# An identity tile built on VectorE, and weight sums taken from tiles that are still on the chip

## Chip, cores and metric

The kernel runs on one core of a Trainium2 chip. The metric is the device time of one execution in microseconds (us), as the median of several runs. The engines are TensorE (PE; its weight loads are listed as PEld), VectorE (DVE), ScalarE (ACT), GpSimd (POOL) and SyncE (SP), which here only issues DMAs. Every engine works through its instructions in order.

## What is computed

An attention with a feature map, and behind it two feed-forward networks. Cut to what matters:

```python
def _attn_ref(q, k, v, w_phi):          # q, k, v: (4, 8, 576, 64), w_phi: (64, 128)
    def phi(x):
        proj = np.einsum('bhsd,df->bhsf', x, w_phi)
        proj = proj - np.max(np.abs(proj), axis=-1, keepdims=True)
        return np.concatenate([np.exp(proj), np.exp(-proj)], axis=-1)
    q_p, k_p = phi(q), phi(k)
    kv = np.einsum('bhsf,bhsd->bhfd', k_p, v)
    z = np.sum(k_p, axis=2)
    num = np.einsum('bhsf,bhfd->bhsd', q_p, kv)
    den = np.einsum('bhsf,bhf->bhs', q_p, z)[..., None] + 1e-06
    return num / den
# x = attention output as (2304, 512)
r = np.maximum(x @ w_in, 0.0)                      # first network, w_in (512, 2048)
x = (r * r) @ w_out                                # w_out (2048, 512)
gate = 1.0 / (1.0 + np.exp(-(x @ w_gate)))         # second network, w_gate, w_val (512, 1536)
out = gate * (x @ w_val) @ w_out2
```

The inputs `moe_w_in`, `moe_w_out` and so on arrive as 64-bit floats; the kernel makes 32-bit ones of them on the chip ("conversion").

## The kernel before

*Attention* (`actx`, lines 213 to 484). Sixteen iterations `n`, each for a batch and a pair of heads. Tiles of q, k and v are loaded on SP's queue two to three iterations ahead (`load`, L261 to L269, and for the last 64 rows of k and v `load_rem`, L251, L255), transposed on PE with the tile `ident` as the moving operand (`trans_q` L292, `trans_k` L285, `trans_rem` L300), projected (`proj_q` L313, `proj_k` L334), and multiplied. The maximum over the features of q is taken by POOL's `partition_all_reduce` (L318), and used on DVE by `q_exp` (L324).

Before the first iteration (lines 223 to 245) `make_identity` makes `ident` on POOL, with a fill (masks.py:197) and a select (masks.py:199). `w_phi` is loaded on ACT's queue, split into `wq` and spread into `wk` on DVE (L96, L97, L231 to L241). Then PE runs eight matmuls of `ident` by itself (L245), whose result nobody reads, and the transposes of the first iteration follow.

*First network.* 2304 tokens are three blocks of 768. The first block is computed straight (lines 787 to 806, steps `s` = 0 to 17): `h0_step(s)` makes hidden chunk `s` (L517; ACT L520 to L522, DVE L523: a high and a low half, `ghi` and `glo`), and `o1_step(0, s-2)` adds chunk `s-2` into the output (L538). Every fp32 product is made of three passes over high and low halves. A chunk's weights come from DRAM into a `wf` tile (`fetch`, L197; six buffers, fetched two steps ahead) and are split on ACT (L138) and DVE (L139) into `hl`.

The other blocks use a Strassen-Winograd scheme (`chain`, L590): it needs, beside the weights, four sums of each pair of weight pieces (`s1` to `s4`), which lie in DRAM in `wsm` (`ismd`), one tile for two pairs.

*Conversion* (`weight`, lines 105 to 118; `convert1`, 144 to 150). A piece is loaded as 64-bit data on SP (L108, 512 KB), made into a 32-bit tile `a` on DVE (L112, L113, L114, L117) and ACT (L116), in one of four buffers `wpa`, and stored to DRAM on SP: a piece of `w_in` into `half` (L147, `wid`), a piece of `w_out` into `parked` (L133, `wd`). The order is in, in, out, out for each pair. Ten pieces are converted during the attention (`CONVERTING`): the input pieces 0 to 5 and the output pieces 0 to 3. The rest follow in steps 0 to 12 of the first block (`converts1`), at 7 pieces for 4 steps.

*Sums* (`sums`, lines 159 to 167; `in_sums`, 169 to 178). For each of eight pairs of input pieces, in steps 3, 5, ..., 17, `in_sums` fetches both pieces back from DRAM into two `wf` tiles (L176), makes the four sums on DVE (L163 to L166) in the one buffer `s`, and stores them on SP (L167). For the second network `convert2` already makes its sums from the converted tiles, kept in `kept` until the pair is there.

*What sets the order.* The code is written in program order; a scheduler then puts each engine's instructions in order by a timeline simulation of its own. `tc.issue_after(last_g[0].ins)` places what is traced inside it behind the latest `glo` (or similar) on that instruction's engine.

Of the kernel before, what the change touches and what calls it, by code (L numbers as in the profile page):

```python
# [9 lines left out]

F32 = mybir.dt.float32
# [3 lines left out]
ALU = mybir.AluOpType  # L15
# [5 lines left out]
def attention_moe_moe2(ctx, tc, q, k, v, w_phi, w_in, w_out, w_gate, w_val, w_out2, out):  # L21
    nc = tc.nc
# [3 lines left out]
    P = 128  # L26
# [11 lines left out]
    C1 = w_in.shape[1] // P  # L38
# [5 lines left out]
    CONVERTING = (1, 2, 3, 4, 5, 6, 7, 8, 10, 12)  # L44
# [8 lines left out]
    wpa = ctx.enter_context(tc.tile_pool(name="wpa", bufs=NWA))  # L53
# [30 lines left out]
    def col_src(w, c):  # L84
        return w[:, c * P:(c + 1) * P].rearrange("(j p) f -> p j f", p=P)

    def row_src(w, c):
        return w[c * P:(c + 1) * P, :].rearrange("p (j f) -> p j f", j=NJ)
# [16 lines left out]
    def weight(pool, src):  # L105
        a = pool.tile([P, NJ * P], F32, tag="w", name="w")
        st = raw.tile([P, NJ, P], src.dtype, tag="st", name="st")
        nc.sync.dma_start(out=st, in_=src)  # L108
        u = st.rearrange("p j f -> p (j f)").bitcast(U32).rearrange("p (n t) -> p n t", t=2)
        lo, hi = u[:, :, 0], u[:, :, 1]  # L110
        b = a.bitcast(U32)
        nc.vector.tensor_scalar(b, hi, 3, 0x3FFFFFF8, ALU.logical_shift_left, ALU.bitwise_and)  # L112
        nc.vector.scalar_tensor_tensor(b, hi, 0xC0000000, b, ALU.bitwise_and, ALU.bitwise_or)  # L113
        nc.vector.scalar_tensor_tensor(b, lo, 29, b, ALU.logical_shift_right, ALU.bitwise_or)  # L114
        h = hi.bitcast(F32)
        nc.scalar.activation(h, h, AF.Square)  # L116
        nc.vector.scalar_tensor_tensor(a, h, TINY, a, ALU.is_ge, ALU.mult)  # L117
        return a
# [4 lines left out]
    wsm = [dr.tile([P, 4, 2, HF], F32, tag=f"is{q}", name="ismd") for q in range(C1 // 4)]  # L123
    parked = {}

    def in_piece(c):
        q, r = divmod(c, 4)
        return half[2 * q + r % 2][:, r // 2]

    def park(key, a):  # L130
        if key not in parked:
            parked[key] = dr.tile([P, NJ * P], F32, tag=f"d{len(parked)}", name="wd")
        nc.sync.dma_start(out=parked[key], in_=a)  # L133
# [10 lines left out]
    def convert1(k):  # L144
        o, c = order1[k]
        if o == "in":
            nc.sync.dma_start(out=in_piece(c), in_=weight(wpa, col_src(w_in, c)))  # L147
        else:
            park(("o1", c), weight(wpa, row_src(w_out, c)))
        done.add((o, c))  # L150

    done = set()
    gvd = [dr.tile([P, 2, NJ * P], F32, tag=f"gv{c}", name="gvd") for c in range(C2)]
    smd = [dr.tile([P, 4, 2, HF], F32, tag=f"sm{p}", name="smd") for p in range(C2 // 2)]
    order2 = [(c, o) for p in range(C2 // 2) for o in range(2) for c in (2 * p, 2 * p + 1)]
    order2 += [(c, 2) for c in range(C2)]
    kept = {}

    def sums(a, b, dst):
        a11, a12, a21, a22 = a[:, :HF], a[:, HF:], b[:, :HF], b[:, HF:]  # L160
        t = sp.tile([P, 4, HF], F32, tag="s", name="s")
        eng = nc.vector.tensor_tensor
        eng(t[:, 0], a21, a22, ALU.add)  # L163
        eng(t[:, 1], t[:, 0], a11, ALU.subtract)
        eng(t[:, 2], a11, a21, ALU.subtract)
        eng(t[:, 3], a12, t[:, 1], ALU.subtract)  # L166
        nc.sync.dma_start(out=dst, in_=t)  # L167

    def in_sums(i):
        q, m = divmod(i, 2)  # L170
        ab = []
        for k in range(2):
            c = 4 * q + 2 * m + k
            assert ("in", c) in done
            t = wf.tile([P, NJ * P], F32, tag="wf", name="wf")
            nc.sync.dma_start(out=t, in_=in_piece(c))  # L176
            ab.append(t)
        sums(*ab, wsm[q][:, :, m])
# [21 lines left out]
    def fetch_for(s):  # L200
        if s < C1:
            assert {("in", s), ("out", s)} <= done
            fetch(("in", s), in_piece(s))
            fetch(("out", s), parked["o1", s])

    def split_in(s):
        if s < C1 and ("in", s) not in ws:
            wsplit(("in", s), fetched.pop(("in", s)))

    def split_out(s):  # L210
        wsplit(("out", s), fetched.pop(("out", s)))

    with ExitStack() as actx:
        cst = actx.enter_context(tc.tile_pool(name="cst", bufs=1))
# [6 lines left out]
        sm = actx.enter_context(tc.tile_pool(name="sm", bufs=2))  # L221

        ident = cst.tile([P, P], F32, name="ident")
        make_identity(nc, ident)
        wst = cst.tile([P, F], F32, name="wst")
        for e in range(2):
            nc.scalar.dma_start(out=wst[e * D:(e + 1) * D, :], in_=w_phi)
# [10 lines left out]
        for x in range(2):  # L238
            for e in range(2):
                sl = slice(e * D, (e + 1) * D)  # L240
# [268 lines left out]
    def h0_step(c):  # L509
        w = ws.pop(("in", c))  # L510
        gs[c] = pair()
        pp = dbl()
        for i, (o, n) in enumerate(HALVES):
            k = 0
            for j in range(NJ):
                for x, y in passes:
                    nc.tensor.matmul(pp[:, i, :n], lhsT=w[:, x, j, :], rhs=xs[j][:, y, o:o + n], start=k == 0, stop=k == 3 * NJ - 1)  # L517
                    k += 1
        r, sq = scr(), scr()
        nc.scalar.activation(r, pp[:, :, :NH], AF.Relu)  # L520
        nc.scalar.activation(gs[c][0], flat(r), AF.Square)
        nc.scalar.activation(sq, r, AF.Square)  # L522
        last_g[0] = nc.vector.tensor_tensor(gs[c][1], flat(sq), f(gs[c][0]), ALU.subtract)  # L523
# [31 lines left out]
    def xop(t, k):  # L555
        def h(d, j):
            return xy[t, d][:, :, j * NH:(j + 1) * NH]

        def minus(x, y):
            d = scr()  # L560
            nc.vector.tensor_tensor(d, x, y, ALU.subtract)
            return d

        with tc.issue_after(last_g[0].ins):
            if k == "T2":
                diff["T1"] = minus(h(0, 1), h(0, 0))
                src = diff["T2"] = minus(h(1, 1), diff["T1"])
            elif k == "T3":
                src = minus(h(1, 1), h(0, 1))
            elif k == "T4":  # L570
                src = minus(h(1, 0), diff.pop("T2"))
            elif k == "T1":
                src = diff.pop("T1")
            else:
                src = h(*{"B11": (0, 0), "B21": (1, 0), "B22": (1, 1)}[k])
            i = HOME.index(k)
            a = (xp if i < 4 else xb).tile([P, 2, 2, NH], F32R, tag=f"xo{i}", name="xs")
            split(a[:, 0], a[:, 1], src, nc.scalar)
        xs[k] = a
# [174 lines left out]
    def run_ahead(k, nf, nsp):  # L754
        nonlocal done_f, done_s
        while done_f < min(len(seq), k + nf):
            fetch(seq[done_f][0], seq[done_f][1]())
            done_f += 1
        while done_s < min(len(seq), k + nsp, done_f):
            key = seq[done_s][0]  # L760
            wsplit(key, fetched.pop(key))
            done_s += 1
# [6 lines left out]
    def converts1(s):  # L769
        nonlocal nc1  # L770
        with tc.issue_after(last_g[0].ins):
            while nc1 < min(NW1, nw + (7 * (s + 1) + 3) // 4):
                convert1(nc1)
                nc1 += 1
# [3 lines left out]
    def converts2(at):  # L778
        nonlocal nc2
        upto = int(NW2 * (at + 6) / (moe2 + 36))  # L780
        with tc.issue_after(last_g[0].ins):
            while nc2 < min(upto, NW2):
                convert2(nc2)
                nc2 += 1

    fetch_for(1)
    for s in range(C1 + 2):
        if s < C1:
            fetch_for(s + ahead)
            h0_step(s)  # L790
            split_in(s + 1)
        if 1 <= s <= C1:
            split_out(s - 1)
        for i, k in ((C1 - 5, "B11"), (C1 - 4, "B21"), (C1 - 3, "T2"), (C1 - 1, "T3"), (C1 - 1, "T1"), (C1, "B22"), (C1, "T4")):
            if s == i:
                xop(1, k)
        if s >= C1 - 1:
            run_ahead(0, 5, 0 if s < C1 else 3)
        if s >= 2:
            o1_step(0, s - 2, ws.pop(("out", s - 2)))  # L800
        if s < C1:
            converts1(s)
        if s >= 3 and s % 2 and s <= C1 + 1:
            for i in range(C1 // 2):
                if i == (s - 3) // 2:
                    in_sums(i)

    for k, (at, fn, *args) in enumerate(acts):
        run_ahead(first[k], 11, 6)
        fn(*args)  # L810
        converts2(at)
# [30 lines left out]
```

## Time and profile before

| | |
|---|---|
| median of three runs | 1026.83 us (1023.62 to 1028.88) |
| the profiled execution | 1027.08 us, span 1025.3 us |
| PE busy | 992.4 us, 97% of the span |
| PEld, DVE, ACT, POOL busy | 85%, 73%, 59%, 11% |
| HBM read, written | 127.99 MB, 33.03 MB |
| chain of work that ended last | PE 85%, DVE 6%, DMA 4%, ACT 2%, issue 2% |

The span runs from the first to the last instruction; all times below are counted from its start. A busy share is a share of the span. In the timeline a row gives start, duration, engine, line, operation, tiles and shapes, and in brackets how long the engine had stood before it and what ended that. Waits are put down to the release that came last. "<-issue" is time in which the engine waited for nothing that the profile shows.

### The profile page before, as it was taken

To read this page: it belongs to the slowest core of one execution; us is meant where nothing else is said; L and a number is where in the kernel's file an instruction comes from. 1 tells how busy PE (TensorE), PEld (TensorE's weight loads), DVE (VectorE), ACT (ScalarE), POOL (GpSimd) and SP (SyncE) were. 2 spreads that over 40 slices of the span, in tenths; PEclk is the share of its full clock that TensorE was granted. 3 is DMA by queue.
4 is the path that set the end of the run, shared out by engine and by line. 5 is a ranking of instruction groups with operands and counts; after the bars stand their busy time and mean duration, and the time that the engine had idled before them with its cause. 6 is when DMAs were issued, how large, how long until landed. Compare 5 with 4: busy or idle time off the path is not lost.

```text
span 1025.3 us, 17544 instructions
## 1 busy us (share of the span) xinstructions
PE 992.4 (97%) x6488; PEld 870.3 (85%) x6488; DVE 746.6 (73%) x1283; ACT 601.0 (59%) x1081; POOL 109.4 (11%) x198
## 2 busy tenths in 40 slices
PE   5999999999999899999999999999999999999996
PEld 5666666599999799889998899998899988899985
DVE  4799999869875797887968869866566656566542
ACT  4988888546545487545875457654465544455431
POOL 3555665400000000000000000000000000000000
PEclk9999999999999899999999999999999999999999
DMA  8345421339876478457584565642354422544302
GB/s 225 103 142 153 144 92 46 124 119 352 286 270 211 160 246 267 154 167 243 187 282 160 175 187 175 198 139 73 89 158 133 125 93 62 154 133 124 103 13 61
DMA packets 117846, 162.18 MB, mean 158 GB/s; under 512 B 12928, under 2 KB 75008, under 8 KB 117760
## 3 DMA queue, kind: packets, MB, share of 16 engines
q1 hardware_dynamic: 117120, 160.20, 49.8%
q8 instruction: 51, 0.84, 0.3%
q10 hardware_dynamic: 640, 0.85, 0.2%
q14 instruction: 35, 0.29, 0.1%
HBM read 127.99 MB, written 33.03 MB: 157 GB/s over the span
## 4 chain that ended last, share of the span: by engine, by line
PE 85%; DVE 6%; DMA 4%; ACT 2%; issue 2%; POOL 0%; ACTq 0%; SPq 0%; POOLq 0%; DVEq 0%
PE d L590 37%; PE d L538 17%; PE d L694 15%; PE d L517 4%; PE a L360 3%; DMA wf<-wid 2%; PE a L397 2%; PE a L334 2%; PE a L367 1%; PE a L390 1%; PE a L313 1%; DMA st<-in_moe_w_in_dram 1%; PE a L292 1%; DVE km L339 1%; PE a L377 1%
## 5 line engine op out<-in xcount | busy, mean ns | idle before, releaser
L590 PE MATMUL d<-xs,hl 128*128 128x384 f32 x2184 | 385.5, 337 | 3.6 <-ACT c L596 3.6
L590 PEld LDWEIGHTS d<-xs,hl 128*128 128x128 f32 x2184 | 379.5, 188 | 6.7 <-ACT c L596 4.9
L139 DVE TENSOR_TENSOR hl<-wf,hl 128x512 fp32r<-128x512 f32 x282 | 192.5, 688 | 76.4 <-ACT hl L138 75.3
L138 ACT ACTIVATE hl<-wf 128x512 fp32r<-128x512 f32 x282 | 174.9, 625 | 94.4 <-PE d L590 47.5
L538 PE MATMUL d<-ghi,hl 128*128 128x256 f32 (+1 forms) x768 | 191.9, 340 | 0.0
L538 PEld LDWEIGHTS d<-ghi,hl 128*128 128x128 f32 x768 | 133.0, 190 | 16.4
L538 PE MATMUL d<-glo,hl 128*128 128x512 f32 (+1 forms) x384 | 130.0, 342 | 5.1 <-DVE glo L523 5.1
L694 PE MATMUL d<-hl,ghi 128*128 128x512 f32 x432 | 126.7, 395 | 0.0
L94 ACT ACTIVATE ghi<-G 128x768 fp32r<-128x768 f32 x48 | 40.7, 847 | 99.3 <-PE d L694 56.0
L694 PEld LDWEIGHTS d<-hl,ghi 128*128 128x128 f32 x432 | 80.9, 188 | 18.2
L97 DVE TENSOR_TENSOR glo<-G,ghi 128x768 fp32r<-128x768 f32 x48 | 46.0, 958 | 57.3 <-ACT ghi L94 56.9
L596 ACT ACTIVATE c<-d 128x768 f32<-128x768 f32 x78 | 61.3, 809 | 44.7 <-PE d L590 44.5
L318 POOL PARTITION_ALL_REDUCE m<-qe x64 | 82.5, 1359 | 28.5 <-ACT qe L316 26.8
L538 PEld LDWEIGHTS d<-glo,hl 128*128 128x128 f32 x384 | 73.1, 190 | 14.1 <-DVE glo L523 5.4
L619 DVE TENSOR_TENSOR c<-c,d 128x768 f32<-128x768 f32 x54 | 51.2, 953 | 41.1 <-ACT c L596 26.8
L694 PE MATMUL d<-hl,glo 128*128 128x512 f32 x216 | 76.3, 395 | 0.0
L517 PE MATMUL d<-xs,hl 128*128 128x384 f32 x384 | 69.2, 337 | 2.1 <-DVE u L417 1.7
L517 PEld LDWEIGHTS d<-xs,hl 128*128 128x128 f32 x384 | 66.6, 188 | 3.8 <-DVE u L417 2.2
L116 ACT ACTIVATE st<-st 128x512 f32<-128x512 f32 x68 | 45.7, 680 | 37.0 <-DVE w L113 34.2
L694 PEld LDWEIGHTS d<-hl,glo 128*128 128x128 f32 x216 | 40.6, 188 | 9.8
L113 DVE SCALAR_TENSOR_TENSOR w<-st,w 128x512 uint32<-128x512 uint32 x68 | 48.0, 718 | 0.3
L117 DVE SCALAR_TENSOR_TENSOR w<-st,w 128x512 f32<-128x512 f32 x68 | 46.3, 687 | 1.4 <-ACT st L116 0.5
(105 smaller groups left out, 1128.3 us busy)
## 6 DMA issues: line engine op xcount, KB each, us to landing
wf<-wd SPq DMA_DIRECT2D x84, 256.0 KB, 3.0
wf<-smd SPq DMA_DIRECT2D x72, 256.0 KB, 3.0
st<-in_moe_w_out_dram SPq DMA_DIRECT2D x28, 512.0 KB, 5.0
wf<-wid SPq DMA_DIRECT2D x56, 256.0 KB, 4.6
wf<-gvd SPq DMA_DIRECT2D x54, 256.0 KB, 3.1
st<-in_moe_w_in_dram SPq DMA_DIRECT2D x16, 512.0 KB, 5.1
wf<-ismd SPq DMA_DIRECT2D x32, 256.0 KB, 3.5
wd<-w SPq DMA_DIRECT2D x28, 256.0 KB, 3.3
```

The costliest lines, as they stand in the source:

```text
L97: last_g[0] = nc.vector.tensor_tensor(lo, src, f(hi), ALU.subtract)
L113: nc.vector.scalar_tensor_tensor(b, hi, 0xC0000000, b, ALU.bitwise_and, ALU.bitwise_or)
L117: nc.vector.scalar_tensor_tensor(a, h, TINY, a, ALU.is_ge, ALU.mult)
L138: nc.scalar.activation(d[:, 0], a, AF.Copy)
L139: nc.vector.tensor_tensor(d[:, 1], a, f(d[:, 0]), ALU.subtract)
L318: nc.gpsimd.partition_all_reduce(m, a[:, 1, :], channels=P, reduce_op=bass_isa.ReduceOp.absmax)
L517: nc.tensor.matmul(pp[:, i, :n], lhsT=w[:, x, j, :], rhs=xs[j][:, y, o:o + n], start=k == 0, stop=k == 3 * NJ - 1)
L538: nc.tensor.matmul(acc[j][i], lhsT=w[:, x, j, :], rhs=a[y][:, o:o + n], start=c == 0 and k == 0 and (i == 0 or j % 2 == 0), stop=c == C1 - ...
L590: nc.tensor.matmul(acc[k, q][:, m], lhsT=w[:, i, 2 * m + kt, :], rhs=v[:, j, kt, :], start=start and n == 0, stop=n == 5, skip_group_check ...
L596: nc.scalar.activation(side[name, q], acc["X", q], AF.Copy)
L619: nc.vector.tensor_tensor(a, a, acc[k, q], ALU.add)
L694: nc.tensor.matmul(acc[u], lhsT=g[x][:, u * P:(u + 1) * P], rhs=w[:, y].rearrange("p j f -> p (j f)"), start=c == 0 and n == 0, stop=c == ...
```

## The change

Two things are changed. `ident` is no longer made on POOL. On DVE it is filled with zeros; a ramp 0 to 31 is made along the free dimension by five additions, each doubling what is there; `transpose` turns it within blocks of 32x32, so that each row holds its own number; a comparison of the two gives an identity of 32x32 in each group of 32 partitions; and four copies put these on the diagonal of `ident`.

And in the first network, when the second piece of a pair of input pieces is converted inside `converts1` (from the eleventh conversion on), `sums` is called at once with the two converted tiles, and the pair is marked as done. Only pairs that are not done are still made by `in_sums`, now in steps 2, 4, 6 and 8.

```diff
-from concourse.masks import make_identity
@@ convert1
         if o == "in":
-            nc.sync.dma_start(out=in_piece(c), in_=weight(wpa, col_src(w_in, c)))
+            a = weight(wpa, col_src(w_in, c))
+            nc.sync.dma_start(out=in_piece(c), in_=a)
+            kept[c] = a
+            if k >= len(CONVERTING) and c % 2:
+                sums(kept[c - 1], a, wsm[c // 4][:, :, c % 4 // 2])
+                done.add(("sum", c // 2))
         else:
             park(("o1", c), weight(wpa, row_src(w_out, c)))
         done.add((o, c))
@@
         ident = cst.tile([P, P], F32, name="ident")
-        make_identity(nc, ident)
+        ramp = cst.tile([P, 3, 32], F32, name="ramp")
+        nc.vector.memset(ident, 0.0)
+        nc.vector.memset(ramp[:, 0, 0:1], 0.0)
+        for n in (1, 2, 4, 8, 16):
+            nc.vector.tensor_scalar(ramp[:, 0, n:2 * n], ramp[:, 0, :n], float(n), None, ALU.add)
+        nc.vector.transpose(ramp[:, 1], ramp[:, 0])
+        nc.vector.tensor_tensor(ramp[:, 2], ramp[:, 0], ramp[:, 1], ALU.is_equal)
+        for i in range(4):
+            sl = slice(32 * i, 32 * i + 32)
+            nc.vector.tensor_copy(ident[sl, sl], ramp[sl, 2])
@@ the loop over the steps s
-        if s >= 3 and s % 2 and s <= C1 + 1:
-            for i in range(C1 // 2):
-                if i == (s - 3) // 2:
-                    in_sums(i)
-
+        if s in (2, 4, 6, 8) and ("sum", s // 2 - 1) not in done:
+            in_sums(s // 2 - 1)
+
+    kept.clear()
```

## Rows read from the trace of the kernel before

**Rows 1.** Stages: length, busy us of PE, PEld, DVE, ACT, POOL; clock, DMA, GB/s.

```profile
100.00:203.90 103.90, 101.07 (x1158) 63.76 (x1156) 92.76 (x208) 80.54 (x196) 58.99 (x115) 1.00 0.33 104
203.90:278.00 74.10, 73.74 (x422) 69.68 (x423) 59.49 (x106) 39.58 (x59) 0.00 (x0) 1.00 0.73 252
278.00:338.00 60.00, 59.64 (x339) 54.81 (x337) 38.09 (x65) 30.54 (x45) 0.00 (x0) 1.00 0.72 231
...
341.00:348.00 7.00, 4.90 (x16) 4.22 (x17) 6.69 (x10) 3.09 (x4) 0.00 (x0) 0.51 0.80 260
```

**Rows 2.** PE's waits after 200 us: us in total, times, longest.

```profile
PE d L590 <- ACT c L596: 3.6, 4, 0.9
```

**Rows 3.** Timeline of the start.

```profile
0.80 0.09 DVE L231 MEMSET ones<- 128x32 f32 x1 [0.80 <-PEq L826]
0.86 0.17 DVE L233 MEMSET zr<- 128x128 f32 x1
...
2.16 0.75 SPq L251 DMA_DIRECT2D kr<-in_k_dram  x1
...
4.92 0.45 SPq L264 DMA_DIRECT2D k<-in_k_dram  x1
...
9.43 0.28 POOL masks.py:199 TENSOR_SCALAR_AFFINE_SELECT ident<-ident 128x128 f32<-128x128 f32 x1 [8.51 <-issue]
...
9.76 3.74 PE L245 MATMUL a<-ident 128*128 128x128 f32 x16 [9.76 <-POOL ident masks.py:199]
...
13.34 0.66 PE L292 MATMUL a<-ident,q 96*128 96x96 f32 x6
...
13.84 0.60 PE L285 MATMUL a<-ident,k 128*128 128x128 f32 x4
...
16.00 4.95 POOL L318 PARTITION_ALL_REDUCE m<-qe  x4 [6.29 <-ACT qe L316]
...
17.83 0.66 PE L292 MATMUL a<-ident,q 96*128 96x96 f32 x6
...
19.26 0.45 DVE L324 TENSOR_TENSOR qe<-qe,m 128x288 f32<-128x288 f32 x1
```

**Rows 4.** Timeline at the end of the first network's first block.

```profile
332.53 0.83 ACT L521 ACTIVATE ghi<-c 128x768 fp32r<-128x768 f32 x1
...
333.83 0.43 DVE L163 TENSOR_TENSOR s<-wf 128x256 f32<-128x256 f32 x1 [4.00 <-DMA wf<-wid]
...
339.54 0.42 DVE L163 TENSOR_TENSOR s<-wf 128x256 f32<-128x256 f32 x1 [4.16 <-DMA ismd<-s]
...
342.10 0.95 DVE L523 TENSOR_TENSOR glo<-c,ghi 128x768 fp32r<-128x768 f32 x1
...
343.10 0.80 PE L538 MATMUL d<-glo,hl 128*128 128x512 f32 x1 [5.07 <-DVE glo L523]
```

**Rows 5.** Chain that ended last: start, us, what; two stretches of 21 matmuls.

```profile
343.10 6.02 PE d L538 x21
...
470.06 3.65 PE d L538 x21
```

**Rows 6.** DVE groups by shape: busy us, mean ns, idle before.

```profile
L401 DVE STREAM_TRANSPOSE den<-a 128x288 f32<-128x288 f32 x16 | 7.6, 475 | 1.2 <-PE a L390 1.1
L403 DVE TENSOR_SCALAR rd<-den 128x9 f32<-128x9 f32 x16 | 2.6, 165 | 0.1
```

**Rows 7.** DMA issues from 2.1 to 5.35 us: count, KB, median us to landing.

```profile
k<-in_k_dram SPq DMA_DIRECT2D x1, 256.0 KB, 4.7
kr<-in_k_dram SPq DMA_DIRECT2D x1, 128.0 KB, 5.0
```

**Rows 8.** Timeline: the splits for one step, and PE's use of them.

```profile
245.47 1.29 DVE L139 TENSOR_TENSOR hl<-wf,hl 128x512 fp32r<-128x512 f32 x2
...
247.53 4.33 PE L517 MATMUL d<-xs,hl 128*128 128x384 f32 x24
```

**Rows 9.** DMA issues from 204 to 345 us, the stores of the sums.

```profile
ismd<-s SPq DMA_DIRECT2D x8, 512.0 KB, 4.6
```

More of the change, by code (lines that the diff above doesn't have):

```diff
@@ L152, in attention_moe_moe2 @@
     done = set()
+    kept = {}
     gvd = [dr.tile([P, 2, NJ * P], F32, tag=f"gv{c}", name="gvd") for c in range(C2)]
@@ L156, in attention_moe_moe2 @@
     order2 += [(c, 2) for c in range(C2)]
-    kept = {}
     def sums(a, b, dst):
```

## The prediction

> **What bounds the kernel now.** I read the stages first: busy time of each engine in stretches of the span. In each of them TensorE (PE) is close to full: 101.07 of 103.9 us late in the attention, 73.74 of 74.1 in the first network up to 278 us, 59.64 of 60 up to 338 [rows 1]. So nothing is gained by making VectorE (DVE) or the queues cheaper as such; a gain must come from a place where PE stands still. The second view is therefore the list of PE's waits. After 200 us it holds one large entry, at 343 us; the next is four waits at L590 with 3.6 us in sum, which the change does not touch [rows 2]. Before 200 us the large one is the very start, where PE waits 9.76 us for the identity tile. I then read the timeline around both.
>
> *The start.* POOL fills the tile at once, but its select (the second half of the identity) starts only at 9.43 us, after 8.5 us in which POOL waits for nothing that the profile shows; PE's warm-up matmuls (L245) start at 9.76 and take 3.74 us, and the first transposes follow at 13.34 without a gap [rows 3]. The 16 warm-up passes take 234 ns apiece, four transposes of the same shape just behind them 150 ns [rows 3]: they are the price of raising the clock, and come wherever PE starts.
>
> *The end of the first network's first block.* PE stops at 338.03 and takes up L538 at 343.10, after 5.07 us, for the low half of the last hidden chunk (`glo`, L523). Its input was ready on ScalarE (ACT) by 333.36 (332.53 plus 0.83), but on DVE's in-order queue two weight-sum groups (L163) stand ahead of it, one held 4.00 us by its reloaded tile, the next 4.16 us by the landing of the previous sums, which still occupy the single `s` buffer [rows 4]. During the stop the granted clock falls: it is 0.51 over 341 to 348 us, so mostly the lower of the two levels, 1.2 GHz [rows 1]. The 21 matmuls after the stop take 6.02 us, 21 like them elsewhere 3.65 [rows 5].
>
> **Part 1, the identity on DVE.** Removed: POOL's fill and select, and with them the 8.5 us on PE's path. Added: 13 DVE instructions, in order on one engine, which is idle until 0.80 us [rows 3]: a fill of 128x128 (like L233, 0.17 us), a fill of one column (at most like L231, 0.09), five additions on 1 to 16 columns, a 32-column transpose, a comparison, four 32x32 copies. The trace shows none of the last eleven. The nearest row for a very short operation is 165 ns (128x9, L403); the transpose it shows has nine times the columns, from PSUM, and takes 475 ns [rows 6]. At 165 ns for all eleven: 0.17 + 0.09 + 11 x 0.165 = 2.08 us, tile ready at 2.9. Bounds: 13 x 0.085 = 1.1 us (tile at 1.9), or 475 ns for transpose and comparison, 2.7 us (3.5). I take 2.9, since nearly all of them are as short as L403's. The DVE work pushed back, the clearing of `wk`, has cover: its next step waits for a load until well after that.
>
> Warm-up then runs 2.9 to 6.65 instead of 9.76 to 13.50: 6.85 us earlier. What is late next? Loads do not depend on the identity, so they keep their times. The remainder tile of k, issued at 2.16, lands 5.0 us later, at 7.2; the k tile of the second pair, issued at 4.92, after 4.7 us, at 9.6 [rows 3, 7]. PE wants the first after its ten leading transposes, which end at 14.44 now and at 7.6 then, and the second shortly after 17.83, then 11.0 [rows 3]: covered by 0.4 and 1.4 us. POOL's first all-reduce starts at 16.00, then 9.15; its result is used on DVE at 19.26, then 12.4 [rows 3]. If POOL has a start-up of the same 8.5 us ahead of its first such instruction, counted from its first arrival there (0.9), it is free at 9.4 and the first of four results (4.95/4 = 1.24 us) is there at 10.6, still before 12.4. From there the attention is paced by PE [rows 1], so the lead stays: **-6.85 us** (bounds -6.2 and -7.8, from the DVE bounds).
>
> The Trainium skill speaks against this step: its "GPSIMD Engine Reference", Instruction dispatch, has the first call of a freshly loaded kernel pay a code load of about 6 us without a visible instruction. The 8.5 us agree in kind, not in size; whether the all-reduce pays it again, and when it begins, no row shows. By the page's figure, begun at arrival, the sum stays; begun at the call, most of this part goes. That is rival B.
>
> **Part 2, the sums.** Of the eight pairs the first three still reload (their six input pieces are converted in the attention), each one step earlier. Pairs 3 to 7 are summed as soon as their second piece is converted, by program order in steps 1, 4, 6, 8 and 10 rather than 9 to 17. Removed: ten reloads of 256 KB, ten issues on SyncE's queue (SP), their claims on the `wf` buffers, and DVE's waits for them. Not removed: 4 DVE operations of 0.42 us for each pair, and the store. The store is now on SP directly behind the piece's own, and waits up to 4 x 0.42 = 1.7 us for the sums; behind it queue the next weight loads and the fetches for the next step. The converted tiles stay in their four buffers until the sums have read them, no longer than their own store roughly takes.
>
> At 333 us no sum stands ahead of `glo` any more: it can follow at 333.4, done 0.95 us later, 3.7 us before PE needs it. So the stop goes, 5.07 us, and so does the low clock, 6.02 - 3.65 = 2.37 us: **-7.44 us**. Next late there would be the split of the first chain's weights, but these fetches stood behind the same reloads on SP, and DVE loses 8.2 us of waiting and three sums in that stretch.
>
> The cost lies earlier. DVE is busy 59.49 of 74.1 us from 203.9 to 278 [rows 1]; three more sums fall there, 5.1 us, so 64.6 of 74.1. The cover is thin: the split of a step's weights (x2) ends at 246.76, its first half some 0.6 us earlier, and PE takes it at 247.53 [rows 8], so 0.8 to 1.4 us. Bounds: 0 (DVE has 9.5 us to spare and fewer loads to wait for) and 5.1 us (all of it arrives at PE). I take **+1 us**, nearer to nothing, because DVE is not full and a late conversion has two steps of room, but not nothing, because of the thin cover.
>
> **The sum.** 6.85 + 7.44 - 1 = 13.3 us off the profiled execution's 1027.08 us (span 1025.3): 1013.8. The median of the runs is 0.25 us lower, so **1013.5 us**. With the bounds of the DVE price and the pile-up, 1011.6 to 1018.3.
>
> **Rivals.** *B: POOL's start-up moves instead of going.* If it begins only when the first all-reduce has its input, it runs 9.15 to 17.65, the first result comes at 18.9, and DVE's in-order queue stands from 12.4 to there: 6.5 of the 6.85 us are lost. Time 1027.08 - 0.35 - 6.44 = 1020.3, or 1020. For: the select too was preceded by this gap. Against: the all-reduce that exists now starts at 16.00 on the word of its input (ACT, L316), with no gap of its own behind that [rows 3]. Chance 0.12.
>
> *C: the stop at 343 us stays in another form*, say because the order in which work is put on DVE's queue, made anew for the changed program, places other work ahead of `glo`, or SP fetches late. Only part 1 remains: 1027.08 - 6.85 + 1 = 1021.2, or 1021. For: DVE's queue at that point also carries splits for the second block. Against: both long waits there belong to the sums. Chance 0.13.
>
> *D: slower.* Two sums now meet in one step (pairs 0 and 3, 1 and 4, 2 and 5). With one `s` buffer the second must wait until the first has landed, 4.6 us in the median [rows 9]; DVE stands meanwhile with the splits of the next step behind it. A meeting then costs PE up to 4.6 + 1.7 - 1.4 = 4.9 us, about the stop that pulled the clock down, so with the clock 4.9 + 2.4 = 7.3. Three of them: 21.9 us, and 1027.08 - 14.3 + 21.9 = 1034.7. It takes 14.3 us to use up the gain, so it decides from 4.8 us at each of three meetings. Against: the scheduling can put the second sum behind the splits. Chance 0.08.
>
> *E: no difference*, through milder meetings together with B or C: 1024 to 1029, chance 0.07.
>
> **How the numbers follow.** The forecast has 0.60. Half a per cent, about what a measurement of this kernel can tell from no change, is 5.1 us: faster is below 1021.7. The forecast (0.60), B (0.12) and most of C (0.09 of 0.13) lie there: 0.81. Same: E and the rest of C, 0.11. Slower: D, 0.08. For the range: from 1008, the best bound 1011.6 less the 3.2 us by which the lowest run lies under the median (1023.62 under 1026.83), to 1022, which takes in B and C and leaves out D and E.
>
> **What would show it.** Right: the identity's last copy on DVE near 2.9 us, L245 right behind it, L292 near 6.6; POOL's first all-reduce near 9.2; the first network's start (now at 203.9) near 197; no PE wait on `glo` and the clock at its upper level through the change of block; ten fewer L176 issues. Wrong: a gap on POOL between the first input and the first all-reduce (B); PE waits on `glo` or `hl` near the change of block (C); DVE waits of 4 us on `ismd<-s` between 205 and 270 us with PE waiting on `hl` behind them (D). The prediction falls as a whole if the attention, started earlier, doesn't end earlier.

## The result, and the profile after

The changed kernel takes 1012.93 us (median of four runs, 1012.71 to 1013.1) against 1026.11 for the kernel before (four runs, one more than above; 1023.62 to 1028.88); the ratio is 0.9871, 95% interval 0.9844 to 0.9897. The forecast was 1013.5, 1008 to 1022. In the profiled executions the span goes from 1025.3 to 1011.3 us, 14.0 less. Line numbers move: what was L245, L292, L313, L377, L397, L417 is L258, L305, L326, L390, L410, L430; L517, L523, L538, L590 are now L530, L536, L551, L603; the sums L163 to L167 are L167 to L171, the fetch L197 is L201.

The start, from the timeline of the changed kernel (columns as in [rows 3]):

```profile
1.09 0.10 DVE L232 TENSOR_SCALAR ramp<-ramp 128x1 f32<-128x1 f32 x1
...
1.21 0.36 DVE L250 CAST wk<-zr 128x128 fp32r<-128x128 f32 x2
1.48 0.16 DVE L232 TENSOR_SCALAR ramp<-ramp 128x2 f32<-128x2 f32 x1
1.55 0.35 DVE L250 CAST wk<-zr 128x128 fp32r<-128x128 f32 x2
...
1.82 0.58 DVE L232 TENSOR_SCALAR ramp<-ramp 128x4 f32<-128x4 f32 x3
...
2.43 0.21 DVE L233 STREAM_TRANSPOSE ramp<-ramp 128x32 f32<-128x32 f32 x1
2.68 0.19 DVE L234 TENSOR_TENSOR ramp<-ramp 128x32 f32<-128x32 f32 x1
2.90 0.73 DVE L237 COPY ident<-ramp 32x32 f32<-32x32 f32 x4
...
3.69 3.78 PE L258 MATMUL a<-ident 128*128 128x128 f32 x16 [3.69 <-DVE ident L237]
...
7.26 0.98 PE L305 MATMUL a<-ident,q 96*128 96x96 f32 x6
...
10.19 4.91 POOL L331 PARTITION_ALL_REDUCE m<-qe  x4 [9.76 <-ACT qe L329]
```

PE begins at 3.69 us instead of 9.76 [rows 3], the first all-reduce at 10.19 instead of 16.00, and at once when its input is there. The ramp's steps are not alone on DVE: four casts for `wk` stand among them.

PE's waits after 198 us are down to one kind (us in total, times, longest), the one that the change doesn't touch [rows 2]:

```profile
PE d L603 <- ACT c L609: 3.6, 4, 0.9
```

Stages of the changed kernel around the places that moved (columns as in [rows 1]), from two answers:

```profile
24.90:28.40 3.50, 3.50 (x20) 2.78 (x18) 3.04 (x6) 3.18 (x10) 0.16 (x1) 0.51 0.86 194
...
198.40:272.00 73.60, 73.60 (x423) 69.52 (x422) 61.21 (x114) 39.70 (x58) 0.76 (x5) 1.00 0.75 257
272.00:335.00 63.00, 63.00 (x362) 58.49 (x361) 45.41 (x74) 34.44 (x51) 0.00 (x0) 1.00 0.64 209
```

PE is busy without a break from the first network's first matmul to the end of its first block, at the upper clock level, although DVE is fuller than before in the first of the two stretches. The low clock over 24.9 to 28.4 us is new; a repeated run of the same program, further down, does not have it. The sums, asked for by their tile (x: how many; first and last start):

```profile
L167 DVE TENSOR_TENSOR s<-w x5: 417/421/425, 224.2 to 292.8; 128x256 f32<-128x256 f32 x5
L167 DVE TENSOR_TENSOR s<-wf x3: 419/419/420, 232.9 to 272.9; 128x256 f32<-128x256 f32 x3
  DMA ismd<-s: 1.3, 2
```

Five pairs come from converted tiles (`w`), three from reloads (`wf`), all begun before 295 us, and DVE waited for the `s` buffer 1.3 us in all. The transfers `wf<-wid` are 46, before 56. Two points of the chain that ended last give the rest of the account, with the first network's first matmul in the timeline of the kernel before and of the changed one:

```profile
198.51 12.68 PE d L530 x72
...
334.89 49.92 PE d L603 x288
```

```profile
204.26 12.77 PE L517 MATMUL d<-xs,hl 128*128 128x384 f32 x72 [1.74 <-DVE u L417]
```

```profile
198.44 1.83 PE L530 MATMUL d<-xs,hl 128*128 128x384 f32 x9
```

From that matmul to the long run of the second block it is 334.89 - 198.44 = 136.45 us; before, 349.13 - 204.26 = 144.87 (the stop's end at 343.10 and the 6.02 us behind it [rows 5]). So the first network's first block gave 8.4 us, and what lies ahead of it 5.8. Everything after it is as long as before, within 0.25 us.

### The profile page after: what moved, and what is told of

Read it like the earlier page. It is cut to its first block, busy times and chain, and to the rows that moved or that the text cites. A ratio compares the mean times of both kernels' runs of the same rounds, so it can differ in the third digit from the quotient of the medians.

```text
span 1011.3 us, 17524 instructions
## 1 busy us (share of the span) xinstructions
PE 991.6 (98%) x6488; PEld 870.3 (86%) x6488; DVE 747.3 (74%) x1296; ACT 601.7 (59%) x1081; POOL 109.7 (11%) x196
## 4 chain that ended last, share of the span: by engine, by line
PE 94%; DVE 3%; ACT 2%; POOL 0%; issue 0%; ACTq 0%
PE d L603 38%; PE d L551 20%; PE d L707 15%; PE d L530 7%; PE a L373 3%; PE a L410 3%; PE a L347 2%; PE a L380 2%; PE a L403 2%; PE a L326 1%; PE a L305 1%; PE a L390 1%; PE a L298 1%; ACT qe L329 0%; PE a L258 0%; ACT c L609 0%
## 5 line engine op out<-in xcount | busy, mean ns | idle before, releaser
L603 PE MATMUL d<-xs,hl 128*128 128x384 f32 x2184 | 385.4, 337 | 3.6 <-ACT c L609 3.6
L603 PEld LDWEIGHTS d<-xs,hl 128*128 128x128 f32 x2184 | 379.4, 188 | 6.6 <-ACT c L609 4.9
L551 PE MATMUL d<-ghi,hl 128*128 128x256 f32 (+1 forms) x768 | 190.7, 338 | 0.0
L551 PEld LDWEIGHTS d<-ghi,hl 128*128 128x128 f32 x768 | 131.8, 188 | 16.3
L551 PE MATMUL d<-glo,hl 128*128 128x512 f32 (+1 forms) x384 | 128.5, 338 | 0.0
L551 PEld LDWEIGHTS d<-glo,hl 128*128 128x128 f32 x384 | 72.3, 188 | 8.6
L530 PE MATMUL d<-xs,hl 128*128 128x384 f32 x384 | 69.1, 337 | 0.0
L530 PEld LDWEIGHTS d<-xs,hl 128*128 128x128 f32 x384 | 66.7, 188 | 1.1 <-issue 0.4
L112 DVE SCALAR_TENSOR_TENSOR w<-st,w 128x512 uint32<-128x512 uint32 x68 | 46.6, 698 | 0.2
L113 DVE SCALAR_TENSOR_TENSOR w<-st,w 128x512 uint32<-128x512 uint32 x68 | 46.4, 693 | 0.5
```

The costliest lines, as they stand in the source:

```text
L551: nc.tensor.matmul(acc[j][i], lhsT=w[:, x, j, :], rhs=a[y][:, o:o + n], start=c == 0 and k == 0 and (i == 0 or j % 2 == 0), stop=c == C1 - ...
L603: nc.tensor.matmul(acc[k, q][:, m], lhsT=w[:, i, 2 * m + kt, :], rhs=v[:, j, kt, :], start=start and n == 0, stop=n == 5, skip_group_check ...
```

## The experiments

**Each part alone.** Only the identity (the diff's `ident` part on the kernel before):

> The kernel before with the identity made on VectorE and nothing else. Theory (the two parts add up): TensorE starts near 3.7 us instead of 9.76, the first network starts near 198.4 instead of 204.26, and the stop of about 5 us with the low clock behind it stays at the end of the first block; 5.8 us faster than before, about 1020.3 us. Rival (the order of work made anew after any change is what removes the stop): the stop is gone here too, and the time is near 1013 us.

Measured: 1020.21 us against 1026.19 on the same chip, ratio 0.9944 (0.9929 to 0.9958). PE's waits and the chain at the end of the block (L547 is L538, L532 is L523, L599 is L590):

```profile
PE d L547 <- DVE glo L532: 5.1, 1, 5.1
```

```profile
336.24 6.00 PE d L547 x21
342.24 49.92 PE d L599 x288
```

The stop stays, with its low clock. The span is 1018.5, 6.8 less: the first network starts at 198.16, 6.1 us earlier, and its first block takes 342.24 - 198.16 = 144.08 us, 0.8 less than before although its sums are as before. Only the sums (the changed kernel with `make_identity(nc, ident)` in place of the ramp):

> The changed kernel with the identity put back on GpSimd, so that only the sums from converted tiles are left of the change. Theory: TensorE starts at 9.8 us, the first network at about 204.3, no wait for glo at the end of the first block, which ends near 340.7 instead of 349.1 us; 8.2 to 8.4 us faster, about 1018 us. Rival (the stop goes only because the earlier start of the attention moved the loads): the stop stays, 1024 us or more.

Measured: 1019.88 us, ratio 0.9938 (0.9922 to 0.9955), so 6.3 us, two less than expected. The chain, with the span at 1018.0, that is 7.3 less (L522 is L517, L595 is L590), and the start:

```profile
204.99 12.75 PE d L522 x72
...
341.44 49.92 PE d L595 x288
```

```profile
9.93 0.28 POOL masks.py:199 TENSOR_SCALAR_AFFINE_SELECT ident<-ident 128x128 f32<-128x128 f32 x1 [9.01 <-issue]
```

The block is again 341.44 - 204.99 = 136.45 us, to the hundredth that of the changed kernel, with no wait for `glo`: the sums do their 8.4 us without the identity. Of the two us missing in the medians 0.7 lie ahead of the block, where POOL's gap before the select was 9.01 us and 8.51 before, and 0.4 behind it. Most of the last 1.0 is the choice of executions: the profiled one of the kernel before took 1027.08 us, the median on this chip is 1026.19. Within the scatter of the runs the two parts add: 6.0 + 6.3 = 12.3 us in the medians, against 13.2 together, and 6.8 + 7.3 = 14.1 in the spans, against 14.0.

**Has the all-reduce a start-up?** The changed kernel with, ahead of all others,

```diff
+        pz0 = cst.tile([P, F], F32, name="pz0")
+        nc.gpsimd.partition_all_reduce(pz0, zr, channels=P, reduce_op=bass_isa.ReduceOp.absmax)
```

> The changed kernel with one more all-reduce on GpSimd ahead of all others, of a tile of zeros that is ready at about 1.2 us; its result is not used. Theory (the all-reduce has a start-up of its own, about as long as the 8.5 us before the select, begun when GpSimd arrives at it): this all-reduce starts near 9.0 to 9.7 us, the first real one near 10.7, and the time stays within 1 us of the changed kernel's 1012.9. Rival (the 8.5 us belong to the select alone): it starts near 1.5 us.

and then the same with a reader on DVE, `nc.vector.tensor_copy(pz1, pz0)`:

> The changed kernel with the early extra all-reduce of zeros, now with a copy on VectorE that reads its result. It tells whether that all-reduce, shown at 1.26 us, really ended then. Theory (the 8.5 us belong to the select, and the all-reduce has no start-up): the copy runs near 2.5 us and the time is within 1 us of 1012.9. Rival (its shown start is early, and a start-up of some 8 us lies inside): VectorE waits for it until 9 us or later, and the time is 4 us or more above 1012.9.

Measured: 1012.93 and 1013.03 us, one run each. From the second's timeline:

```profile
1.27 0.77 POOL L248 PARTITION_ALL_REDUCE pz<-zr  x1 [0.84 <-DVE ramp L232]
...
2.58 0.22 DVE L250 COPY pz<-pz 128x128 f32<-128x128 f32 x1
```

The first all-reduce of the program runs at 1.27 us, and a reader has its result at 2.58. My theory falls: there is no start-up to move. The 8.5 to 9.0 us stood before the select and, as far as these programs show, belong to it. A change from one kind of instruction to another on POOL does not bring such a gap in general: in the kernel before, POOL goes from the all-reduce to copies and back, and each time a release by another engine ends its wait.

```profile
39.11 1.89 POOL L411 COPY rc<-rd 32x9 f32<-32x9 f32 x8 [2.15 <-DVE rd L404]
43.24 5.06 POOL L318 PARTITION_ALL_REDUCE m<-qe  x4 [2.24 <-ACT qe L316]
```

Whether it is the select itself or the change from a fill to it is not separated. The Trainium skill's "GPSIMD Engine Reference", Instruction dispatch, has the first call of a freshly loaded kernel (a piece of code for POOL) pay about 6 us that no instruction in the profile shows. The gap before the select is of that kind but longer, 8.51 and 9.01 us; this all-reduce shows none.

**Is it the place of the sums, or the reload?** The kernel before, with every pair reloaded, but the sums where the changed kernel has them:

```diff
-        if s >= 3 and s % 2 and s <= C1 + 1:
-            for i in range(C1 // 2):
-                if i == (s - 3) // 2:
-                    in_sums(i)
+        for i in {1: (3,), 2: (0,), 4: (4, 1), 6: (5, 2), 8: (6,), 10: (7,)}.get(s, ()):
+            in_sums(i)
```

> The kernel before (identity on GpSimd, all eight pairs reloaded), with each pair's sums only put in the program where the changed kernel has them: steps 1, 2, 4, 4, 6, 6, 8 and 10 instead of 3 to 17. It tells the place of the sums from the reload. Theory (the place decides: sums stood ahead of the last glo on VectorE's queue): the stop at the end of the first block goes although nothing is saved in traffic, 7 to 8 us faster, about 1018.5 us. Rival (the reloads decide, through the queue of SyncE and the buffers): a stop stays or comes earlier, less than 4 us faster, 1022 us or more.

Measured: 1040.09 us, 13.9 slower, ratio 1.0135 (1.012 to 1.015). Its waits of PE, those of SP's queue, and the first stop in the timeline:

```profile
PE d L517 <- ACT hl L138: 14.8, 4, 7.3
```

```profile
SPq L176 <- DMA wid<-w: 7.1, 8, 2.3
...
SPq L147 <- DVE w L112: 4.4, 1, 4.4
```

```profile
228.93 0.32 SPq L147 DMA_DIRECT2D wid<-w  x1
...
231.26 0.32 SPq L176 DMA_DIRECT2D wf<-wid  x1
231.63 0.42 SPq L197 DMA_DIRECT2D wf<-wid  x1
...
237.15 1.15 ACT L138 ACTIVATE hl<-wf 128x512 fp32r<-128x512 f32 x2 [4.21 <-DMA wf<-wid]
...
237.84 1.01 PE L517 MATMUL d<-xs,hl 128*128 128x384 f32 x2 [7.30 <-ACT hl L138]
```

The reload (L176) of a piece can't go before the piece is converted and its store (L147) has landed, and the fetch of the next step's weights (L197) stands behind it on SP's in-order queue. It is issued at 231.63, and its split comes 7.3 us too late for PE. In the kernel before the same fetch, the fifth of `wf<-wid`, goes out at 190.78, with no reload ahead of it. The landing is the small part of the wait: the store waited 4.4 us for the conversion, the reload behind it 1.0 us for the store. Why the scheduler keeps the fetch behind the reload (the order of the program or the six `wf` buffers) is not shown. The stop at the end of the block is gone, as the theory said; four stops of 14.8 us in sum have come earlier, with three falls of the clock (to 0.51, 0.57 and 0.57 in stretches of 4 to 7 us). The place alone is no gain.

Then the other way: pairs 5 to 7 behind the block.

```diff
+        if s in (3, 5, 7, 9, 11):
+            in_sums((s - 3) // 2)
+        if s == C1 + 1:
+            with tc.issue_after(last_g[0].ins):
+                for i in range(5, C1 // 2):
+                    in_sums(i)
```

> The kernel before (identity on GpSimd, all pairs reloaded), with the sums of pairs 5, 6 and 7 put only behind the last step of the first block, and on VectorE behind the latest split traced there, so that they can't stand ahead of the last glo. Theory (the stop came from sums standing ahead of glo on VectorE's queue): no wait for glo at the end of the block and no fall of the clock there, 7 to 8 us faster than before, about 1018.5 us, with every reload kept. Rival (the reloads hold up the fetches on SyncE's queue wherever they are, as they did when they were put early): a stop on hl or on the sums appears at the end of the block or in the second block, 1022 us or more.

Measured: 1027.58 us, ratio 1.0013 (1.0004 to 1.0022). PE's waits, and the stretch in which they fall:

```profile
PE d L590 <- ACT hl L138: 3.9, 4, 1.6
```

```profile
352.00:368.00 16.00, 11.88 (x51) 9.75 (x50) 11.81 (x21) 10.90 (x17) 0.00 (x0) 0.89 0.70 233
```

`glo` is no longer waited for, but in the 16 us from 352 on PE is busy 11.88 and the clock falls again: the splits of the second block's weights now come late, among the reloads and sums. What the stop gave is given back some 15 us later. So none of the three places tried for these reloads is free: early they hold the fetches, late the next block, and between them `glo`. Of the versions run, only the one that sums the tiles while they are on the chip, and so takes the reload out, gains from an early place.

**What is next late at the start?** In the changed kernel the warm-up waits for the identity, though it needs no particular data. On the tile of zeros, cleared near 1.1 us:

```diff
-            nc.tensor.matmul(warm, lhsT=ident, rhs=ident, start=True, stop=True)
+            nc.tensor.matmul(warm, lhsT=zr, rhs=zr, start=True, stop=True)
```

> The changed kernel with the warm-up matmuls on the tile of zeros that is cleared near 1.1 us, instead of on the identity. Theory (with the identity early, the warm-up itself stands on the path: it ends at 7.47 while q is there by 3.9, k by 5.0 and the identity by 3.7): warm-up runs from about 1.3 to 5.1, the transposes start near 5.1, the rest of k (7.2) is next late; 1 to 2 us faster than the changed kernel's 1012.9. Rival (the next loads or the weights of the projection set the pace): within 0.5 us of 1012.9.

Measured: 1014.99 us, 2 slower than the changed kernel's median and than its version with the early all-reduce on the same chip (1013.03, one run), although PE started its transposes at 4.80 instead of 7.26. From PE's timeline, and two stretches behind it:

```profile
1.23 3.78 PE L258 MATMUL a<-zr 128*128 128x128 f32 x16 [1.23 <-DVE ramp L232]
...
198.23 2.21 PE L530 MATMUL d<-xs,hl 128*128 128x384 f32 x9 [2.11 <-DVE u L430]
```

```profile
196.00:199.50 3.50, 1.39 (x9) 1.27 (x8) 2.99 (x8) 0.00 (x0) 0.77 (x5) 1.00 0.00 0
199.50:203.00 3.50, 3.50 (x13) 3.50 (x12) 0.14 (x1) 0.00 (x0) 0.00 (x0) 0.51 0.00 0
```

The attention ended earlier, and the first network then stood 2.11 us for the last pair's product on DVE (`u`, L430) and ran at the low clock behind that. The kernel before has a wait of 1.7 us at this place, the changed kernel none: there the first L530 runs at 198.44, ahead of that product (199.78), so it does not need the product's data. I put the wait down to the PSUM banks that the scheduler gives to the first `d` tile, which the product may still be reading; no view shows the banks. Without any warm-up (the loop at L258 left out):

> The changed kernel without the warm-up matmuls. It measures what the warm-up is worth once the identity is early. Theory (the low clock then falls on the transposes and projections of the first iteration, about 3.8 us of work at half speed, 1.9 us lost, against 3.8 us of warm-up saved, of which loads take back some): between 0 and 2 us faster than 1012.9. Rival (the price of raising the clock comes back whole or more, as the first iteration's work has gaps): 1 us or more slower than 1012.9.

Measured: 1012.6 us (1011.94 to 1014.46), the same as with it. Two more numbers of warm-up matmuls on zeros, `NWARM` 6 and 10, whose first L530 waits for an earlier DVE instruction, and the changed kernel beside them:

> The changed kernel with warm-up on the tile of zeros, and six warm-up matmuls instead of eight. In this program the first L530 of the first network waits for an earlier instruction of VectorE than in the run with eight, which waited 2.1 us for the last pair's product (the first d tile took over PSUM that this product still read). Theory (in the run with eight, the 2 us that the attention won were lost at this hand-over, by that wait and the low clock from 199.5 to 202.9 us): no PE wait before the first L530, which starts near 196.2, no fall of the clock there, and 1009.5 to 1010.5 us. Rival (the attention itself gives the early start back): the first L530 near 198, 1012 to 1013 us.

> As the kernel with six warm-up matmuls on zeros, with ten; its first L530 too waits for an earlier instruction of VectorE. Theory: as there, with the warm-up ending some 0.9 us later than with eight, near 5.9 us, still before the rest of k (7.2): the first L530 near 196.5, 1009.5 to 1011 us. Rival: near 198, 1012 to 1013 us.

> The changed kernel once more, on the same chip as the two with warm-up on zeros, to compare them with it. Every theory: 1012.9 us, within 0.5.

Measured, on one chip: 1011.24 (1010.47 to 1013.55), 1010.84 (1010.55 to 1011.88) and 1012.68 us (1012.47 to 1012.97). With ten, the first network's start in the chain, and the same two stretches as above:

```profile
195.87 12.94 PE d L530 x72
```

```profile
196.00:199.50 3.50, 3.50 (x20) 3.20 (x20) 3.13 (x8) 0.00 (x0) 0.56 (x3) 1.00 0.00 0
199.50:203.00 3.50, 3.50 (x22) 3.50 (x21) 0.00 (x0) 0.00 (x0) 0.00 (x0) 1.00 0.00 0
```

No wait and no low clock at the hand-over, and 1.8 us under the changed kernel: with ten the theory of the hand-over holds, and it is the best version here. Six missed its forecast in the median. It had no wait at the hand-over either, but its profiled execution gave the rival's picture: its matmuls were slow until about 13.9 us, and L530 came at 198.93. The same ten matmuls of the first iteration, with six and with ten:

```profile
10.25 2.50 PE L347 MATMUL a<-wk,kT 128*128 128x256 f32 x10
```

```profile
8.95 1.44 PE L347 MATMUL a<-wk,kT 128*128 128x256 f32 x10
```

Its other runs took 1010.5 to 1011.8 us.

## Why the prediction was right, point by point

*Part 1: -6.85 forecast, -5.8 in the spans, -6.0 alone.* Two terms of the sum were off, and a third that I did not have made up for most of it. The signs named for this part came 0.7 to 1.4 us late: L305 at 7.26 for 6.6, the first all-reduce at 10.19 for 9.2, the first network at 198.44 for 197.

- The DVE price. Each operation costs about what L403 promised: 0.10 to 0.21 us for steps, transpose, comparison and copies. But the tile is ready at 3.63, not 2.9, and later than the 3.5 that was to be the bound: "in order on one engine" took the 13 for alone there, and the scheduler put `ones`, `zr` and the four casts of `wk` among them. The term is 2.8 us instead of 2.1.
- "From there the attention is paced by PE, so the lead stays" failed. The lead is 6.07 us at the warm-up, 20.05 - 14.69 = 5.4 at the second iteration's first projections (L334, L347), 29.08 - 24.05 = 5.0 at the first transposes of `kvt` and 198.12 - 194.11 = 4.0 at the last. These transposes before, in the changed kernel, and in its repeated run:

```profile
29.08 0.44 PE L377 MATMUL a<-ident,kvt 128*128 128x128 f32 x2 [0.74 <-ACT kvt L369]
...
198.12 0.55 PE L377 MATMUL a<-ident,kvt 128*128 128x128 f32 x3
```

```profile
24.05 0.44 PE L390 MATMUL a<-ident,kvt 128*128 128x128 f32 x2 [1.40 <-ACT kvt L382]
...
194.11 0.55 PE L390 MATMUL a<-ident,kvt 128*128 128x128 f32 x3
```

```profile
24.59 0.44 PE L390 MATMUL a<-ident,kvt 128*128 128x128 f32 x2 [1.41 <-ACT kvt L382]
...
193.57 0.55 PE L390 MATMUL a<-ident,kvt 128*128 128x128 f32 x3
```

  Of the first 0.7 us lost, 0.3 are the first six transposes, which took 0.98 us instead of 0.66; the rest I have not divided. Another 0.3 went where the chain that ended last runs over ACT and not PE, from 18.3 to 29.0 us before and from 13.2 to 24.0 in the changed kernel. The last 1.0 is the low clock behind the wait of 1.40 us (the first row of the stages above): between the two transposes lie 170.1 us, in the repeated run, which waited as long and whose clock did not fall there, 169.0, and before 169.0. The repeated run had lost more at its start and kept 198.12 - 193.57 = 4.6.
- The wait of 1.7 us at the start of the first network, which I listed nowhere, went away, by a change in the scheduled order or the PSUM banks that nobody aimed at. That was luck: 4.0 + 1.7 = 5.7, and with 0.1 by which the matmul now overlaps the one before it, 5.8.

*POOL.* The prediction assumed a start-up of 8.5 us before the first all-reduce and hid it by 1.8 us. There is none, so rival B had no ground. The right answer came from a wrong premise. Rival B's own "against", the first all-reduce that started on the word of its input, spoke against the gap, and I did not carry it over to the forecast.

*Part 2: -7.44 forecast, plus 1 for the pile-up; -8.4 measured.* The stop and the low clock went as worked out. One reading was wrong without changing the sum: `glo` needs not only `ghi`, ready at 333.36, but also `c`, which ScalarE finished at 334.09 in the kernel before:

```profile
333.26 0.83 ACT L522 ACTIVATE c<-c 128x768 f32<-128x768 f32 x1
```

In the changed kernel `glo` follows `c` at 327.85, and PE takes it up after 330.66. The pile-up did not come: DVE is busy 61.21 of 73.6 us and PE 73.60, so the price is the lower bound, 0. A further 1.0 us was saved between 204 and 338 us: 0.4 of it is PE's small waits there. It is hardly the sums' doing, as the kernel with only the identity changed has 0.8 of it too; against that kernel the block is 144.08 - 136.45 = 7.6 us shorter, close to the 7.44. The cause of the 1.0 stays open. Rival D was wrong about its buffer: of the 4.6 us at each of three meetings, 1.3 us were waited in two, and PE noticed nothing. But its shape, a wait on an in-order queue with the next step's splits behind it, is what the early reload showed, at 13.9 us.

*The reading of the stop was too simple.* "Both long waits there belong to the sums" is true, and without the rest of the change of no use: sums that reload are late, early or in the way. The prediction lists the removed reloads without a price of their own, and the runs show that the gain hangs on them: with them the same early place cost 13.9 us.

*The sum.* -6.85 - 7.44 + 1 = -13.3 against -14.0 in the spans and -13.2 in the medians. Part 1 gave a us less than forecast, part 2 two more: the sum came closer than its terms, and that too is luck.

## What to carry to other kernels

A step that stands ahead of others on an in-order queue was not cured here by moving it, early or late: ask what it waits for, and whether the data can be taken where they still are. When an early stage is shortened, follow the lead to the next hand-over, by the same instruction in both traces, instead of taking a busy engine for the one that sets the pace. Data-free work such as a warm-up should hang on the first tile that is there, but a gain of 2 us at the start can be lost at the next hand-over, as it was here with eight matmuls and not with ten.

## What the runs showed of the hardware

- The first GpSimd `partition_all_reduce` of a program ran at 1.27 us with its result read at 2.58; the select of `make_identity` came 8.51 and 9.01 us after its fill.
- Very short DVE operations on 1 to 32 columns took 0.10 to 0.21 us each, four 32x32 copies 0.73 together.
- One and the same program ran differently in two executions: its first six transposes behind the same 3.78 us of warm-up took 0.98 us in one and 1.17 in the other, and behind a PE wait of 1.4 us near 23 us the granted clock was 0.51 from 24.9 to 28.4 in one and 1.00 in the other.
- With six warm-up matmuls (2.93 us) PE's matmuls were slow until about 13.9 us in the profiled execution (1.20 us for the first six transposes, 0.69 for the next six at 13.83), without any until 13.1 (1.19 and 0.66). The clock column of the profile reads 1.00 in these stretches all the same, so there the durations tell more than the column.
